# Gating the last tile of a channel-attention kernel into another buffer slot, before its sum is done

## The chip, the cores and the metric

The kernel runs on one core of a Trainium2 chip. The metric is device time in microseconds (us), lower is better. It is measured over several executions, alternating with the kernel before on the same chip.

TensorE is called PE below, VectorE DVE, ScalarE ACT, SyncE SP, as in the profile. PEq, ACTq and SPq are the instruction queues of these engines; loads and stores are issued on the last two.

## The reference, cut to what matters

```
# x: (1, 384, 384, 384) bfloat16, w1d: (1,) bfloat16; k = 1
g = jnp.einsum("bhwc->bc", x) / (H * W)      # mean of each channel
s = _sigmoid(g * w1d[0])                     # one gate per channel
return x * s[:, None, None, :]
```

113.25 MB have to be read and as many written. The gate depends on all of x, and x does not fit on the core.

## The kernel before

A "row" below is 384 channels on each of 128 partitions; x has 1152 of them. The first 12 rows are one small tile; the other 1140 are 19 tiles of 60 rows (5.9 MB each), which go through 4 slots of on-chip memory. To read x only once, the kernel computes an early gate `s_early` from the first 4 rows, multiplies every tile by it and stores it. Meanwhile PE sums all rows (a matmul with ones). At the end the true gate is computed and compared bit for bit with the early one; only if they differ is everything done again.

A tile's life is: load, sum on PE, gate on DVE **in place**, store, and then the slot takes the tile four further on. Because the gate overwrites the tile, it must wait until PE has read it. The helper that does this, and the loop, are:

```python
FIRST, EARLY, TILE, SLOTS, BOTH = 12, 4, 60, 4, 3
# ... cut ...
    def put(place, n, r0):
        plan.op(
            "vector",
            gate(place, place, n, s_early),          # multiply, in place
            reads=["s_early"] + rows(place, n),
            writes=rows(place, n),
        )
        plan.final.append(
            plan.dma("scalar", dram(o_rows, r0, n), at(place, n), reads=rows(place, n))
        )
# ... cut ...
    for k in range(n_tiles):
        if k >= SLOTS:
            put(slot(k), TILE, row0(k - SLOTS))      # gate and store tile k - 4 ...
            load(slot(k), TILE, row0(k))             # ... then load tile k into its slot
        there = rows(slot(k), TILE)
        plan.relay(ready, "gpsimd", "tensor", there, there, ["acc1"])
    plan.signals("tensor", rows(base, FIRST), ["acc1"])
    for k in range(n_tiles - SLOTS, n_tiles):        # the last four tiles
        put(slot(k), TILE, row0(k))
    put(base, FIRST, 0)                              # the small first tile goes last
```

The planner turns `reads` and `writes` into waits on semaphores (counters by which engines wait for one another). Loads are issued on the SP queue (the first ones partly on ACT's), stores on the ACT queue. The sums are closed by three matmuls on zeros after the last tile:

```python
        def emit(e):
            add_rows(e, 1, (base + EARLY) * C, FIRST - EARLY, True, False)
            # ... cut: the loop over all tiles ...
            for i in range(3):
                out = mm(e, acc[1][i][:, :], ones[:], none, False, True)   # none: zeros
            out.then_inc(plan.sems["tensor"], 1)
```

## Time and profile before

| Kernel before | |
|---|---|
| time, median of 3 runs (a fourth came with the result) | 532.6 us (531.52 to 533.25) |
| span of the profiled run | 530.1 us |
| busy: PE, DVE, ACT | 42%, 45%, 1% |
| bytes moved, mean rate | 226.52 MB, 427 GB/s |

The two lines below are from the profile page. Each digit of the first is the busy share of the 16 DMA engines in one of 40 equal slices of the span (9 is 90% or more); the second is what they moved.

```profile
DMA  9999999999999999999999999999999999999978
GB/s 388 426 440 393 445 445 445 414 421 445 445 442 417 421 445 445 442 414 424 445 442 442 410 431 442 445 442 403 435 445 445 438 400 442 445 445 438 401 334 368
```

DMA is the bound: 9s in 38 slices, then 7 and 8. Only at the end do the DMA engines fall short, so that is where something can be had without moving fewer bytes. The Trainium skill ("DMA: Bandwidth & Descriptors", "Where 436 GB/s comes from") puts the ceiling of the 16 engines at 435.2 GB/s; one packet of 46,080 bytes takes 1.702 us, which is 27.1 GB/s for an engine and 433 for 16 of them (slices of 445 come from packets counted in the slice where they start).

The timeline of the end (start, duration, engine, line, operation, count, and in brackets the engine's idle time before it and what released it):

```profile
487.81 11.53 PE L238 MATMUL acc<-arena,ones 128*128 128x512 bf16 x45 [15.97 <-PEq L279]
499.18 0.81 PE L238 MATMUL acc<-zeros,ones 128*128 128x512 bf16 x3
499.38 14.63 DVE L202 TENSOR_TENSOR arena<-arena,s_early 128x23040 bf16<-128x23040 bf16 x2 [15.13 <-PE acc L238]
511.57 2.81 ACTq L109 DMA_DIRECT2D out_dram<-arena  x2
```

PE sums the last tile from 487.8 to 499.2. DVE, idle for 15.13 us, is released by PE, gates the last tile (12.16 us) and the small tile (2.55 us), and the last two stores are issued from 511.57 on. Now the DMA engines around that moment, in the view of stretches (columns: stretch and length in us, busy time of PE, weight loads, DVE, ACT, POOL, granted clock of PE, busy share of DMA, GB/s; a packet counts in the stretch where it starts, so a share can pass 1):

```profile
495.00:508.50 13.50, 4.99 (x24) 0.00 (x0) 9.12 (x1) 0.00 (x0) 0.00 (x0) 0.86 1.01 435
508.50:512.40 3.90, 0.00 (x0) 0.00 (x0) 3.90 (x2) 0.00 (x0) 0.00 (x0) 0.50 0.03 12
512.40:524.00 11.60, 0.00 (x0) 0.00 (x0) 5.30 (x10) 0.61 (x1) 0.00 (x0) 0.50 1.03 445
```

From 508.5 to 512.4 hardly a packet starts: fourteen DMA engines have finished the store before by 509.1, the other two by 510.1 and 511.1, and the last tile's store has not been issued yet.

And the issue table gives the time from issue to landing of the last, small store:

```profile
out_dram<-arena ACTq DMA_DIRECT2D x1, 1152.0 KB, 16.0
```

It waits behind nothing but the last tile's store. One warning: the page's chain of what ended last follows instructions. Here it ends with a check on DVE at 518.6, while the span ends at 530.0 with the landing of a store, which that chain does not show. For the end of this kernel one has to read the landings.

### The profile page before, as it was taken

To read this page: it belongs to the slowest core of one execution; us is meant where nothing else is said; L and a number is where in the kernel's file an instruction comes from. 1 tells how busy PE (TensorE), PEld (TensorE's weight loads), DVE (VectorE), ACT (ScalarE), POOL (GpSimd) and SP (SyncE) were. 2 spreads that over 40 slices of the span, in tenths; PEclk is the share of its full clock that TensorE was granted. 3 is DMA by queue.
4 is the path that set the end of the run, shared out by engine and by line. 5 is a ranking of instruction groups with operands and counts; after the bars stand their busy time and mean duration, and the time that the engine had idled before them with its cause. 6 is when DMAs were issued, how large, how long until landed. Compare 5 with 4: busy or idle time off the path is not lost. (4 is left out here: it accounts for less than half of the span.)

```text
span 530.1 us, 1055 instructions
## 1 busy us (share of the span) xinstructions
PE 221.0 (42%) x854; PEld 0.2 (0%) x2; DVE 240.0 (45%) x38; ACT 2.7 (1%) x4; POOL 0.3 (0%) x6
## 2 busy tenths in 40 slices
PE   0489371080808080807171625253443435261700
PEld 0000000000000000000000000000000000000000
DVE  0239948017170809090808071626253544435390
ACT  1000000000000000000000000000000000000000
POOL 0000000000000000000000000000000000000000
PEclk9899867585858575767676676767575858585955
DMA  9999999999999999999999999999999999999978
GB/s 388 426 440 393 445 445 445 414 421 445 445 442 417 421 445 445 442 414 424 445 442 442 410 431 442 445 442 403 435 445 445 438 400 442 445 445 438 401 334 368
DMA packets 6196, 226.52 MB, mean 427 GB/s; under 512 B 690, under 2 KB 690, under 8 KB 690
## 3 DMA queue, kind: packets, MB, share of 16 engines
q10 hardware_dynamic: 3314, 122.10, 53.3%
q1 hardware_dynamic: 2880, 104.40, 45.8%
q8 instruction: 1, 0.02, 0.0%
q14 instruction: 1, 0.01, 0.0%
HBM read 113.25 MB, written 113.25 MB: 427 GB/s over the span
## 5 line engine op out<-in xcount | busy, mean ns | idle before, releaser
L202 DVE TENSOR_TENSOR arena<-arena,s_early 128x23040 bf16<-128x23040 bf16 (+1 forms) x20 | 233.4, 11678 | 261.0 <-PE acc L238 200.4
L238 PE MATMUL acc<-arena,ones 128*128 128x512 bf16 x849 | 219.9, 423 | 263.6 <-PEq L279 262.4
L346 DVE TENSOR_SCALAR w_scaled<-w_all 128x1 f32<-128x1 f32 x2 | 0.2, 153 | 14.4 <-PE w_all L337 14.4
L337 PE MATMUL w_all<-w_one,ones 1*128 1x1 bf16 x1 | 0.2, 158 | 15.4 <-DMA w_one<-in_w1d_dram 15.4
L311 DVE TENSOR_TENSOR total<-total,acc 128x128 f32<-128x128 f32 (+2 forms) x11 | 4.5, 408 | 0.3
L393 ACT ACTIVATE arena<-total,w_scaled 128x384 bf16<-128x384 f32 x1 | 0.6, 614 | 496.3 <-DVE total L311 496.3
L331 ACT ACT_TABLE_LOAD x1 | 1.3, 1283 | 2.3 <-issue 2.3
L309 DVE COPY total<-acc 128x384 f32<-128x384 f32 x1 | 0.6, 557 | 1.2 <-PE acc L238 1.2
L401 DVE TENSOR_TENSOR total<-arena,s_early 128x384 f32<-128x384 uint16 x1 | 0.6, 557 | 0.7 <-ACT arena L393 0.7
L238 PE MATMUL acc<-zeros,ones 128*128 128x512 bf16 x3 | 0.8, 379 | 0.0
L369 ACT ACTIVATE s_early<-total,w_scaled 128x384 bf16<-128x384 f32 x1 | 0.6, 615 | 15.9 <-DVE total L311 15.9
L355 DVE MEMSET ones<- 128x128 bf16 x1 | 0.2, 165 | 1.0 <-PEq L515 1.0
L236 PE MATMUL acc<-arena,ones 128*128 128x512 bf16 x1 | 0.6, 609 | 0.0
L409 DVE TENSOR_REDUCE wrong<-total 128x1 f32<-128x384 f32 x1 | 0.6, 553 | 0.0
L331 ACT ACTIVATE warm<-warm 128x1 f32<-128x1 f32 x1 | 0.2, 203 | 0.0
L415 DVE CAST redo<-wrong 128x1 int32<-128x1 f32 x1 | 0.2, 153 | 0.0
L236 PEld LDWEIGHTS acc<-arena,ones 128*128 128x128 bf16 x1 | 0.1, 105 | 0.0
L337 PEld LDWEIGHTS w_all<-w_one,ones 1*128 1x128 bf16 x1 | 0.1, 98 | 15.3 <-issue 15.3
L515 POOL MEMSET const-bfloat16-1.0<- 128x1 bf16 x1 | 0.1, 101 | 0.0
L515 POOL MEMSET const-uint8-127<- 128x1 uint8 x1 | 0.1, 101 | 0.0
L354 POOL MEMSET zeros<- 128x2 bf16 x1 | 0.1, 99 | 0.0
L353 POOL MEMSET warm<- 128x1 f32 x1 | 0.1, 98 | 0.5 <-POOLq L515 0.5
(2 smaller groups left out, 0.2 us busy)
## 6 DMA issues: line engine op xcount, KB each, us to landing
out_dram<-arena ACTq DMA_DIRECT2D x19, 5760.0 KB, 50.9
arena<-in_x_dram SPq DMA_DIRECT2D x16, 5760.0 KB, 34.2
arena<-in_x_dram ACTq DMA_DIRECT2D x3, 2880.0 KB, 27.5
arena<-in_x_dram SPq DMA_DIRECT2D x3, 2880.0 KB, 36.4
arena<-in_x_dram SPq DMA_DIRECT2D x1, 1152.0 KB, 10.3
out_dram<-arena ACTq DMA_DIRECT2D x1, 1152.0 KB, 16.0
w_one<-in_w1d_dram ACTq DMA_DIRECT2D x1, 0.0 KB
```

Source lines behind the costliest of these rows:

```text
L202: return lambda e: e.tensor_tensor(to_v, v, s_b, ALU.mult)
L236: loaded.append(e.matmul(bank, weights, moving, start=start, stop=stop))
L238: return e.add_instruction(mybir.InstMatmult(name=nc.get_next_instruction_name(), engine=mybir.EngineType.PE, ins=[e.lower_ap(moving), e.l ...
L309: emit = lambda e, part=part, of=of: e.tensor_copy(part, of)
L311: emit = lambda e, part=part, of=of: e.tensor_tensor(part, part, of, ALU.add)
L331: lambda e: e.activation(warm[:, 1:2], warm[:, 0:1], ACT_F.Sigmoid),
L337: lambda e: e.matmul(w_all[:, 0:1], ones[0:1, :], w_one[0:1, 0:1], start=True, stop=True),
L346: lambda e, i=i, n=n: e.tensor_scalar_mul(w_scaled[:, i : i + 1], w_all[:, 0:1], 1.0 / float(P * n)),
L369: lambda e: e.activation(s_early[:], total[:], ACT_F.Sigmoid, scale=w_scaled[:, 0:1]),
L393: lambda e: e.activation(s_true, total[:], ACT_F.Sigmoid, scale=w_scaled[:, 1:2]),
L401: lambda e: e.tensor_tensor(total[:], s_true.bitcast(U16), s_early[:].bitcast(U16), ALU.not_equal),
L409: lambda e: e.reduce_max(wrong[:], total[:], axis=mybir.AxisListType.X),
```

## The change

The last tile (number 18, in slot 2) is gated into slot 3, which held tile 15 and comes free when that tile's store has landed. The gate then no longer overwrites what PE reads, so it needs the load, DVE and the free slot, but not PE. Besides, the last 8 rows of the small tile are split: 4 of them open the sums, and the other 4 close them after the last tile, in place of the three matmuls on zeros (three matmuls either way).

```diff
-    zeros = nc.alloc_sbuf_tensor("zeros", [P, 2], BF16)
 ... cut ...
-            add_rows(e, 1, (base + EARLY) * C, FIRST - EARLY, True, False)
+            add_rows(e, 1, (base + EARLY) * C, 4, True, False)
 ... cut: the loop over the tiles ...
-            for i in range(3):
-                out = mm(e, acc[1][i][:, :], ones[:], none, False, True)
-            out.then_inc(plan.sems["tensor"], 1)
+            add_rows(
+                e, 1, (base + EARLY + 4) * C, FIRST - EARLY - 4, False, True
+            ).then_inc(plan.sems["tensor"], 1)
 ... cut ...
-    def put(place, n, r0):
+    def put(place, n, r0, to=None):
+        to = place if to is None else to
         plan.op(
             "vector",
-            gate(place, place, n, s_early),
+            gate(to, place, n, s_early),
             reads=["s_early"] + rows(place, n),
-            writes=rows(place, n),
+            writes=rows(to, n),
         )
 ... cut: the store reads at(to, n) ...
-    for k in range(n_tiles - SLOTS, n_tiles):
+    for k in range(n_tiles - SLOTS, last):
         put(slot(k), TILE, row0(k))
+
+    put(slot(last), TILE, row0(last), slot(n_tiles))
     put(base, FIRST, 0)
```

More of the change, by code (lines that the diff above doesn't have):

```diff
@@ L206, in bass_standalone__channel_attn_eca__vision_kernel @@
     assert (n_rows - FIRST) % TILE == 0 and base + FIRST < n_arena
-    assert FIRST % 4 == EARLY % 4 == TILE % 4 == 0 and EARLY < FIRST
+    assert FIRST % 4 == EARLY % 4 == TILE % 4 == 0 and EARLY + 4 < FIRST
     last = n_tiles - 1
@@ L274, in sum_others @@
     def sum_others():
-        none = zeros[:, 0:1].broadcast_to([P, WIDE])
         def one(e, s):
@@ L314, in add_banks @@
             plan.op("vector", emit, reads=[f"acc{group}", "total"], writes=["total"])
-    def put(place, n, r0):
+    def put(place, n, r0, to=None):
+        to = place if to is None else to
         plan.op(
             "vector",
-            gate(place, place, n, s_early),
+            gate(to, place, n, s_early),
             reads=["s_early"] + rows(place, n),
-            writes=rows(place, n),
+            writes=rows(to, n),
         )
         plan.final.append(
-            plan.dma("scalar", dram(o_rows, r0, n), at(place, n), reads=rows(place, n))
+            plan.dma("scalar", dram(o_rows, r0, n), at(to, n), reads=rows(to, n))
         )
@@ L353, in bass_standalone__channel_attn_eca__vision_kernel @@
     plan.op("gpsimd", lambda e: e.memset(warm[:, 0:1], 0.0), writes=["warm"])
-    plan.op("gpsimd", lambda e: e.memset(zeros[:], 0.0), writes=["zeros"])
     plan.op("vector", lambda e: e.memset(ones[:], 1.0), writes=["ones"])
@@ L374, in bass_standalone__channel_attn_eca__vision_kernel @@
     )
-    plan.need("tensor", ["zeros"] + rows(base, FIRST))
+    plan.need("tensor", rows(base, FIRST))
     sum_others()
```

## The prediction

> **What bounds the kernel now.** The DMA engines. On the profile page the 16 DMA engines are 90% busy or more in 38 of 40 slices, at 427 GB/s over a 530.1 us span, while DVE is busy 45% and PE 42%. The last two fall short (334 and 368 GB/s); the change aims at them.
>
> **The end of the kernel before, in order** (timeline, chain that ended last, DMA packets of the trace):
> - The last tile's load lands at 487.7. PE sums it from 487.8 to 499.2; the three matmuls on zeros close the sums at 500.0.
> - Only then does DVE gate the tile in place: 499.4 to 511.5 (12.16 us for 128x23040). Its store is issued at 511.57 and its first packet starts at 512.4.
> - The store of the tile before was issued at 484.3. Fourteen DMA engines finish their part between 508.6 and 509.1, the last two at 510.1 and 511.1. So each engine is idle until 512.4: 1.3 us on the slowest, 3.3 to 3.9 us on fourteen, 3.4 us on average.
> - The last tile's store then takes 13.7 us, the first tile's small one 2.8 us, and the span ends with its landing at 530.0. The check of the early gate ends at 518.6, well before.
>
> **What the change does.** The gate of the last tile no longer waits for PE, because it writes another slot. It waits for its load (487.7), for DVE (free at 484.2) and for the store of tile 15 out of that slot, which landed at 480.9. So it should run 487.7 to 499.9, and the store should be issued near 500, some 8.5 us before the first DMA engine has run out of work. The 11.6 us by which the gate moves are thus not the gain; only the DMA engines' idle time is. The gate of the first tile moves to about 500 to 502.5, after PE's last matmul. The three zero matmuls (379 ns each) are replaced by three real ones of the same shape, and one memset of 0.1 us at the start goes: worth nothing here.
>
> The Trainium skill ("DMA: Bandwidth & Descriptors", "Queues, rings and completion order") says that each DMA engine consumes its ring in order. This trace agrees: packets of one store and the next follow within 3 ns. So each engine should run from its part of one store straight into the next. The end is then set by the slowest engine, whose gap is only 1.3 us, not by the average. In this trace one engine falls steadily behind, 2.5 us by the end; if that is a product of profiling, timed runs have less of it and gain up to the 3.4 us.
>
> **Sum.** Gain 1.3 to 3.6 us; I take 2.4. 532.6 - 2.4 = 530.2 us, range 528.5 to 531.8. Faster by over 2%: 1%; within 2%: 98%; slower by over 2%: 1%.
>
> **What would show it.** The gate of the last tile starts at about 487.7, released by a DMA and not by PE, and still takes 12.2 us; its store is issued near 500 and takes longer from issue to landing (about 25 us instead of 16); the DMA share stays at 1.0 from 495 to about 525; the last landings lie 1 us or more apart.
>
> **What would make it wrong.** Gating from one slot to another slower than in place (8 us of slack); the store of tile 15 landing late; DMA engines waiting between stores all the same; scatter larger than the gain (the three runs before differ by 1.7 us).

## More of the kernel before

A profile of one execution comes with each kernel.

Who made DVE wait, over the whole run, is in the view of waits (total us, times, longest):

```profile
DVE arena L202 <- PE acc L238: 200.4, 13, 22.9
DVE arena L202 <- remote: 60.5, 4, 15.2
```

("remote" is a releaser that the view could not place; in the profile after, all such waits are put down to PE.) These 260 us of waiting cost nothing except the last of them: at the other tiles the DMA engines stay busy while DVE waits.

## The result, and the profile after

| | before | after |
|---|---|---|
| median time (4 runs each) | 532.31 us | 528.66 us |
| lowest to highest | 531.52 to 533.25 | 528.48 to 529.79 |
| ratio, 95% interval | | 0.9935 (0.9913 to 0.9957) |
| span of the profiled run | 530.1 us | 527.2 us |

A ratio is the mean time of one kernel's fast runs over that of the other's in the same rounds, so it is not quite the ratio of the medians. Here it stands for 3.5 us (0.65% of 532.3). That is a real gain, but under 2%. The predicted time was 530.2, range 528.5 to 531.8: the result lies inside, at its low edge. That it does owes something to luck: 532.6 less the largest gain predicted, 3.6, is 529.0, and only the half us added to the range on that side takes in 528.66. The forecast of the gain itself ("I take 2.4") was too small.

The profile after, the same views. DMA and GB/s on the page:

```profile
DMA  9999999999999999999999999999999999999997
GB/s 392 425 425 414 440 447 427 413 447 444 434 409 447 444 434 409 447 444 434 416 437 447 437 413 437 447 441 409 437 447 444 409 434 447 444 416 427 442 447 331
```

The slice before the last is at 447 GB/s instead of 334; only the last falls short. The timeline of the end:

```profile
488.76 12.16 DVE L201 TENSOR_TENSOR arena<-arena,s_early 128x23040 bf16<-128x23040 bf16 x1 [3.40 <-DMA arena<-in_x_dram]
488.89 12.18 PE L237 MATMUL acc<-arena,ones 128*128 128x512 bf16 x48 [15.72 <-PEq L276]
500.95 3.08 ACTq L109 DMA_DIRECT2D out_dram<-arena  x2
501.10 2.56 DVE L201 TENSOR_TENSOR arena<-arena,s_early 128x4608 bf16<-128x4608 bf16 x1 [0.19 <-PE acc L237]
```

DVE now waits 3.40 us for the load in place of 15.13 us for PE, and gates while PE sums. Gating into another slot takes the same 12.16 us as in place. The store is issued at 500.95, 10.6 us earlier than before. The stretches:

```profile
495.00:508.50 13.50, 6.06 (x29) 0.00 (x0) 12.18 (x11) 0.61 (x1) 0.00 (x0) 0.90 0.98 424
508.50:512.40 3.90, 0.00 (x0) 0.00 (x0) 0.00 (x0) 0.00 (x0) 0.00 (x0) 0.50 1.12 484
512.40:524.00 11.60, 0.00 (x0) 0.00 (x0) 0.00 (x0) 0.00 (x0) 0.00 (x0) 0.50 0.91 394
```

The hole at 508.5 to 512.4 is gone (0.03 has become 1.12). The 0.91 in the last stretch is no idle time: a packet counts where it starts, and the packets, followed one by one, show all 16 engines at work until the first of them is done at 524.8. The waits and the last store:

```profile
DVE arena L201 <- PE acc L237: 247.0, 18, 25.5
...
DVE arena L201 <- DMA arena<-in_x_dram: 3.4, 1, 3.4
```

```profile
out_dram<-arena ACTq DMA_DIRECT2D x1, 1152.0 KB, 23.5
```

DVE's total wait is almost as long as before (250 us against 261), which shows how little a sum of waits says: only the one before the last tile mattered. And the last store takes longer from issue to landing (23.5 us against 16.0), because it now stands in a full queue: what was a wait on DVE's side has become a wait in the DMA queue, where it leaves no DMA engine idle.

Where did 10.6 us of earlier store turn into about 3 us of time? The packets in the trace answer it. Packets of one DMA engine follow one another within a few ns, so they can be sorted into 16 chains, and the idle time of each chain can be added up. The landings of a transfer come one per engine; the later time is that of the slowest engine. The trace does not say which engine is which across the gap, so the least and most idle time are good to 0.2 us; the mean does not depend on it. Times in us from the span's start:

```
                                   before            after
load of the last tile lands        485.13 to 487.66  485.01 to 488.74
store of the tile before lands     508.92 to 511.58  508.78 to 510.83
idle of the mean DMA engine
  between the last two big stores  3.43              0.00
  (least, most of the 16)          (1.32, 4.01)      (0.00, 0.01)
last store lands                   529.23 to 530.01  525.13 to 527.17
  mean of the 16 engines           529.34            525.80
```

The mean engine is done 3.54 us earlier (529.34 - 525.80), which is nearly the 3.43 us of idle time that went away (the rest fits the packets of the last big store, which took 1.715 us on average after the gap and 1.704 us without one). The last engine is done only 2.84 us earlier (530.01 - 527.17): before, the gap brought all engines into step, since all began the last store at 512.4; after, nothing does, and they end 2.0 us apart instead of 0.8.

### The profile page after: what moved, and what is told of

The parts are those of the page before. It is cut to its first block, busy times and chain, and to the rows that moved or that the text cites. A ratio compares the mean times of both kernels' runs of the same rounds, so it can differ in the third digit from the quotient of the medians.

```text
span 527.2 us, 1066 instructions
## 1 busy us (share of the span) xinstructions
PE 220.1 (42%) x865; PEld 0.2 (0%) x2; DVE 240.1 (46%) x38; ACT 2.7 (1%) x4; POOL 0.3 (0%) x5
## 6 DMA issues: line engine op xcount, KB each, us to landing
out_dram<-arena ACTq DMA_DIRECT2D x1, 1152.0 KB, 23.5
```

## The experiments

Theory D says that the gain is the idle time of the DMA engines between the last two big stores, and nothing else: the wait for the sum hurt only because it let the queue run dry. The rivals: W, the wait for the sum is itself on the path of the end, so that each us by which the last gate starts earlier counts; S, closing the sums in another way is part of the gain; N, the first result was scatter.

Each kernel ran five rounds against the kernel before on the same chip. The eleven runs were in three groups, which share the runs of before: the first four on one chip (before: 531.63 us median), the next four on another (532.66), the last three on a third (532.13). Times scatter upward by several us in some executions of every kernel (before: 530.57 to 538.55 in these groups), so the intervals are about 0.4% wide on either side, and the traces carry more of the argument than the times do. All results were correct.

**The change again.**

> The change itself again, beside its parts on the same chip. Theory D (the gain is DMA idle time between the last two tiles' stores, 3.4 us a DMA engine in the profile before, gone in the profile after): 2.5 to 3.6 us below the kernel before; idle time of the mean DMA engine about 2.7 us, against 5.3 us before. Rival N (the first result was scatter between runs): within 1 us of before.

Measured: 529.17 us median, ratio 0.9939 (0.9900 to 0.9978), thus 3.2 us below before. Its trace has 0.01 us of idle time between the big stores in the mean engine. Over the whole span a mean engine had no packet under way for 3.7 us, against 5.9 in the first profile of before: a fall of 2.2 where 2.6 was expected (the expectation's 2.7 and 5.3 could not be found again by this count). N falls.

**The other slot alone**, with the zeros kept: the `put` and the loop of the diff, without the hunks on `zeros` and `add_rows`.

> The other slot alone, sums still closed by three matmuls on zeros. Theory D: all of the gain, so within 1 us of the changed kernel and 2.5 to 3.6 us below before; last gate starts when the load lands, store issued near 500. Rival S (closing the sums with rows of the first tile is part of the gain): clearly less than the changed kernel's gain.

Measured: 530.04 us median, ratio 0.9957 (0.9917 to 0.9997), thus about 2.3 us below before; 0.01 us of idle time. The time lies below the expected gain, but its interval reaches over that of the whole change. The trace gives a reason for a late end: one engine's last landing came at 528.59, while the mean was 526.05, close to the 525.98 of the change itself on the same chip. By time alone S is not excluded here; by the traces, the two kernels' mean engines end 0.07 us apart.

**The sums alone**: closed by rows of the first tile, last tile in place. Against the changed kernel:

```diff
-    put(slot(last), TILE, row0(last), slot(n_tiles))
+    put(slot(last), TILE, row0(last))        # in place, after its sum
```

> The sums closed by rows of the first tile, but the last tile gated in place after its sum. Theory D: same as before within 1 us; 3 to 4 us of idle time of the mean DMA engine from 508 to 513 as before. Rival S: part of the gain, over 1 us.

Measured: 532.27 us median, ratio 0.9995 (0.9957 to 1.0033): no gain. The idle time is there, though at 2.41 us less than the 3 to 4 expected; in this run the last load landed 1.2 us sooner (486.47), and everything behind it, the last store too, came sooner. With the run before it, this speaks against S: no part of the gain was seen from the sums, though the interval alone would leave room for 2.3 us.

**In place, after the sum, but in two halves.** This is the kernel before with the last tile gated and stored as two pieces of 30 rows.

```diff
-    for k in range(n_tiles - SLOTS, n_tiles):
+    for k in range(n_tiles - SLOTS, last):
         put(slot(k), TILE, row0(k))
+    for i in (0, 30):       # gate rows i to i + 30 in place, then store them
+        ...
```

> The kernel before, in place and waiting for the sum (gate from about 499.4), but the last tile gated and stored in two halves of 30 rows, so the first half's store is issued near 505.5, about 3 us before the first DMA engine runs out of work at 508.5. Theory D: the whole gain, 2.5 to 3.6 us below before, with no idle DMA time at 508 to 513, although the wait for the sum is all there. Rival W (the wait for the sum is itself on the path of the end, so each us by which the last gate starts earlier counts): no gain or a small part, since the gate starts as late as before.

Measured: 530.73 us median, ratio 0.9974 (0.9932 to 1.0015). The trace has no idle time (0.01 us), but this time could not be told from before. So it was run once more in the last group:

> The two halves in place once more, as the first interval (0.9932 to 1.0015) could not tell. Theory D: 1.5 to 3.6 us below before, with no idle DMA time at 508 to 513. Rival W: same as before within 0.5 us.

Measured: 529.04 us median, ratio 0.9939 (0.9902 to 0.9975), 3.2 us below before: the whole gain in this run. Taken together, the two runs of this kernel (0.9974 and 0.9939) put it about 2.3 us below before. The timeline of this run and its stretch at the hole:

```profile
498.66 0.81 PE L238 MATMUL acc<-zeros,ones 128*128 128x512 bf16 x3
498.86 14.70 DVE L202 TENSOR_TENSOR arena<-arena,s_early 128x11520 bf16<-128x11520 bf16 x3 [15.12 <-PE acc L238]
505.05 8.88 ACTq L109 DMA_DIRECT2D out_dram<-arena  x3
```

```profile
508.50:512.40 3.90, 0.00 (x0) 0.00 (x0) 3.90 (x2) 0.00 (x0) 0.00 (x0) 0.50 0.98 419
```

DVE waits 15.12 us for PE as in the kernel before, and starts only 0.5 us sooner than there (498.86). But the first half's store is issued at 505.05, before the queue is empty, and the hole is filled. This speaks against W: the wait is all there, and the gain is too; in both traces of this kernel the mean engine ends as early as with the change (526.03 and 525.89). The Trainium skill ("Perfetto Trace Analysis", "DMA Optimizations") says that splitting DMAs lets some start sooner and may help if the DMA engines are generally idle. Here they were idle for about 1% of the span (5.9 us of 530 in the mean engine, before), and the split helped, because it was at the one place where the queue ran dry.

**The small store ahead of the last big one**, in the kernel before: the store of the first tile, which takes 2.8 us of each engine, fills the gap, and the last tile waits as before.

```diff
+    plan.signals("tensor", rows(base, FIRST), ["acc1"])   # first tile summed, before the loop
 ... cut ...
-    for k in range(n_tiles - SLOTS, n_tiles):
+    for k in range(n_tiles - SLOTS, last):
         put(slot(k), TILE, row0(k))
     put(base, FIRST, 0)
+    put(slot(last), TILE, row0(last))
```

> The kernel before, last tile in place after its sum, but the first tile's small store (2.8 us of every DMA engine) put ahead of the last tile's, so that it fills most of the gap. Same bytes, same waits of the last tile. Theory D: idle time at 508 to 513 falls from 3.4 to about 0.7 us a mean engine, so 2 to 3 us below before. Rival W: no gain, as the last tile's gate and store come as late as before, and now nothing follows: the end would move by at most the 2.8 us of the small store if the last store were on a chain of its own; told from D only by the idle time in the trace, which D puts at 0.7 us.

Measured: 530.15 us median, 2.5 us below the median of before; ratio 0.9968 (0.9912 to 1.0024), so by time alone unclear. The idle time fell to 0.13 us, under the 0.7 expected (the last load landed at 486.30 here, 1.4 us sooner than in the first profile). In the trace the mean engine ends at 526.00, 3.3 us before that of the first profile, and the stretch of the hole is full:

```profile
508.50:512.40 3.90, 0.00 (x0) 0.00 (x0) 3.80 (x5) 0.00 (x0) 0.00 (x0) 0.50 1.11 473
```

**Making the store late on purpose.** In the changed kernel, some rows of the last tile are gated once more, ahead of the whole tile, with the same result. That delays the store by what those rows take on DVE, with no other wait.

```diff
+    plan.op("vector", gate(slot(n_tiles), slot(last), 30, s_early),    # 30, 45, 60 or 60 + 30 rows
+            reads=["s_early"] + rows(slot(last), 30), writes=rows(slot(n_tiles), 30))
     put(slot(last), TILE, row0(last), slot(n_tiles))
```

> The changed kernel with 30 rows of the last tile gated once more ahead of it (same result), which delays its store by about 6.1 us, to 507.1, first packet near 507.9; the first DMA engine runs out of work near 508.4. Theory D: nothing lost, within 1 us of the changed kernel (2.5 to 3.6 us below before). Rival W: about 6 us lost against the changed kernel, or at least its share of it, so at or above before.

> 45 rows gated once more: store delayed by 9.1 us, first packet near 510.9. Theory D: engines that finish near 508.5 idle 2.5 us, those that finish at 510.4 about 0.5 us; 1.9 us a mean engine. If the slowest engine alone sets the end (as predicted), 0.5 us are lost in time; if timed runs follow the mean engine, 1.9 us. So 1 to 3 us below before. Rival W: 9 us lost.

> The whole tile gated twice: store delayed by 12.2 us, first packet near 514.0. Theory D: mean engine idle 5 us, slowest 3.6 us; the gain is gone: 0 to 2 us above before (before had 3.4 us of idle), although the last gate does not wait for the sum. Rival W: the gate starts 11 us earlier than before and the store is issued 1.5 us later, so also about 1 us above before: this run alone does not tell them apart, the three together do (a kink between 6 and 12 us, or a straight line).

> The changed kernel with 60 and 30 rows gated once more: the store is delayed by 18.3 us. From the first three delays: the end is then the chain load, gates, store, 30.8 + 18.3 = 49.1 us after the slowest landing of the last load, against 42.4 before. Theory D with a kink near 9 us of delay: about 9 us above the changed kernel, so 5.5 to 7.5 us above before; idle time of the mean DMA engine 9 to 12 us. Rival W (every us of an earlier gate counts, from the first): 18 us above the changed kernel.

| rows gated more | delay | median | ratio to before (95%) | idle, mean engine | end minus last load's last landing |
|---|---|---|---|---|---|
| 0 (the change again) | 0 | 529.17 | 0.9939 (0.9900 to 0.9978) | 0.01 | 40.12 |
| 30 | 6.1 us | 529.17 | 0.9921 (0.9873 to 0.9969) | 0.75 | 38.97 |
| 45 | 9.1 us | 529.44 | 0.9936 (0.9886 to 0.9985) | 0.65 | 39.86 |
| 60 | 12.2 us | 533.15 | 0.9999 (0.9945 to 1.0054) | 7.81 | 42.85 |
| 90 | 18.3 us | 538.22 | 1.0097 (1.0063 to 1.0132) | 13.09 | 49.04 |

There is a kink, not a line. Six and nine us of delay cost nothing that the times show; 12.2 us cost all of the gain, and 18.3 us cost 9 us against the change (538.22 - 529.17, on two chips), where W had said 18. Against before on the same chip that is 6.1 us by the medians and 5.2 by the ratio. With 45 rows I had expected some of the gain to be lost (1 to 3 us below before) and it was not; the idle time came out at 0.65 us, because the load landed early (487.38) in that run. Its store was issued at 508.79, 8 us later than in the changed kernel, and the hole stayed nearly closed:

```profile
487.40 23.82 DVE L201 TENSOR_TENSOR arena<-arena,s_early 128x17280 bf16<-128x17280 bf16 x3 [3.48 <-DMA arena<-in_x_dram]
508.79 2.81 ACTq L109 DMA_DIRECT2D out_dram<-arena  x2
```

```profile
508.50:512.40 3.90, 0.00 (x0) 0.00 (x0) 3.83 (x5) 0.00 (x0) 0.00 (x0) 0.50 0.92 390
```

With 30 rows the ratio stands for 4.2 us, more than expected, but the medians of that chip differ by 3.5; the 0.75 us of idle time there were not expected, and come with a load that landed late (490.69). The last two columns of the table are those of one execution, which for 30, 60 and 90 rows was a slow one (531.49, 536.61 and 542.08 us). The idle time at 60 and 90 rows (7.81 and 13.09) is above what was expected, because in both profiled runs one DMA engine was far behind (the load's last landing came at 491.96 and 491.03), and all others waited for it. The stretches of the run with 90 rows, in the place where before had its hole, show the queue dry for longer:

```profile
508.50:512.40 3.90, 0.00 (x0) 0.00 (x0) 3.87 (x2) 0.00 (x0) 0.00 (x0) 0.50 0.17 71
512.40:524.00 11.60, 0.00 (x0) 0.00 (x0) 11.60 (x3) 0.00 (x0) 0.00 (x0) 0.50 0.16 68
```

The last column of the table explains the kink. Beyond it, the end is a chain that hangs on the last load: its last landing, the gates, the issue, the first packet 0.85 us after it, the two last stores. With 60 rows that is 42.85 us and with 90 rows 49.04, 6.19 more for 6.1 us more of gating. Taking the delay away again (42.85 - 12.2) leaves an estimate of 30.7 us for the changed kernel, whose end came 38.4 and 40.1 us after that landing in its two profiles: so its chain has 7.7 and 9.4 us to spare, and its end is set by the queue.

**Before against itself.**

> The kernel before against itself, for the scatter of such a comparison. All theories: ratio 1 within 0.4%. If the end is a chain that starts at the landing of the last load on its slowest DMA engine, the profile's span is that landing plus 42.4 us (42.35 in the first profile), whatever the landing is.

Measured: 532.33 us median, ratio 0.9991 (0.9950 to 1.0033), which is the scatter of one such comparison. Its last store landed at 531.14, the last load's last landing was at 488.26: 42.88 us from there to the end, against 42.35 in the first profile and 42.59 with the sums alone, where the hole is too. Of the difference, 0.5 us is PE, which took 12.05 us for the sum here and 11.53 there. So the kernel before hangs on that chain, and the mean engine idled 4.37 us in this run, the slowest 3.25. W is thus right for the first 3 us or so and wrong for the rest: in the kernel before the end does hang on the wait for the sum, but once the gate starts some 3 us sooner, the queue takes over, and a still earlier gate brings nothing.

None of the variants beat the changed kernel clearly. Those without a hole (the slot, the halves, the small store ahead) end, in the mean of the engines, between 525.80 and 526.05 in six profiles, however the hole was closed. That is what theory D demands. The other seven profiles, with a hole or a delay, agree: the mean engine's end less its idle time lies between 525.91 and 526.37 in all of them.

## Why the prediction was right, and where it was off

- *DMA bounds the kernel, and only its idle time can be saved.* Right. The store came 10.6 us earlier and about 3 us were gained; the delays of 6 and 9 us, which cost nothing, and the two halves, which wait for PE in full, show it. The delay of 9 us was expected to cost some of the gain and did not.
- *The gate starts with the landing of the load, takes 12.2 us, and the store is issued near 500.* Right: 488.76, 12.16 us, 500.95. The load landed 1.1 us later than in the first profile, within the slack.
- *Engines run from one store straight into the next.* Right. I had leaned on the Trainium skill ("DMA: Bandwidth & Descriptors", "Queues, rings and completion order") for the ring being consumed in order; the trace after agrees, with 0.01 us of idle time at most on any engine between the two big stores.
- *The closing of the sums is worth nothing.* Right as far as can be told: ratio 0.9995 alone, with an interval of 0.4%; the mean engines with and without it end 0.07 us apart.
- *The last landings lie 1 us or more apart, and the store takes about 25 us from issue to landing.* Right, 2.0 us and 23.5 us.
- *Size: "I take 2.4", and "the end is then set by the slowest engine, whose gap is only 1.3 us, not by the average".* This term was too small. The profiles gave 2.84 us, the timed ratios 3.5 and 3.2 us, about the mean engine's 3.4 us. The step that was off is to take the gap of the engine that was slowest in one trace as what the end gains. Followed along the slowest landings, 1.32 of the 2.84 us are that gap; 0.75 come from the slowest landing of the store before, which was earlier in the profile after (510.83 instead of 511.58), and 0.77 from the time between it and the end, the gap left out (16.34 us instead of 17.11). The lag of an engine is not fixed: in the second profile of before the slowest engine's gap was 3.25 us instead of 1.32. And in the kernel before, a lagging engine holds up the others: the sum cannot start before its part of the last load is there (487.66, while the other 15 had landed by 485.68), and the other engines then idle until the store comes. For these two profiles the balance of the 16 engines adds up: 3.43 us of idle gone, less 0.7 us by which the end is less even (the last engine is now 1.37 us behind the mean, 527.17 - 525.80; before 0.67), leaves 2.7 of the 2.84 us.
- *"If that is a product of profiling, timed runs gain up to the 3.4 us."* The timed runs did gain about that much, but no run here shows whether profiling causes the lag. It stays open. A part of the lag can be seen in the traces: in all 13, one DMA engine also carries a packet of 16 KB of the kind "instruction" between 495.2 and 500.9. It takes 0.93 us, and in the traces where that engine can be followed the packet after it takes 2.1 us instead of 1.7, so the engine falls 1.3 us back. In the two halves and the small store ahead, that is the engine that ends last. The difference between 2.84 and 3.5 us is also within the scatter of single executions.

## What to carry to other kernels

In this kernel, bound by DMA, a wait on a compute engine cost time only where the queue ran dry before the transfer behind that wait was issued. In another such kernel, look for those places by the idle time of the DMA engines, not by the sums of waits, and expect about their length as the gain, not the length of the wait. At the end of a pipeline there is no next tile to cover the last one's processing, so look there first: a free buffer, a last tile in two pieces, or a small independent store put ahead all filled the same hole here. And estimate the gain from the mean of all DMA engines and the evenness of their ends, over more than one trace.

## What the Trainium skill lacked or had wrong

- "DMA: Bandwidth & Descriptors" ("Latency and other measured facts") says that two of the DMA engines are usually slower, and ties that, as a best guess, to software descriptor queues. The loads and stores of this kernel use only the two hardware queues, and in its traces engines lag all the same, in number and amount that change from run to run: at the landing of the last load, one to seven engines are over 1 us behind the first, and the slowest is behind by 2.5 us in the first profile of before, by about 5 us in the run with 60 rows. The kept traces do not number the engines.
- The same page gives about 0.6 us to the first byte on the hardware path. Here the first packet of a store that finds the queue empty starts 0.85 us after the issue begins (511.57 to 512.42; the same within 0.01 us in five other runs). The page does not say from which moment it counts: the issue itself takes 0.34 us, and from its end it is 0.51 us.
- No page looked up gives a number for what an uneven end of the 16 engines costs a kernel bound by DMA: in the changed kernel the last landing comes 2.0 us after the first and 1.37 us after the mean, and the latter, about 0.3% of its time, is what an even end would save (an estimate from that profile).
- "Perfetto Trace Analysis" ("DMA Optimizations") recommends splitting DMAs where the engines are generally idle. It helped here with the engines busy about 99% of the span (3.2 us, 0.6%, in the second run; 0.9974, not clear of noise, in the first), because they were idle in one place.
